# Moving a small transpose, shortening the warm-up and resplitting the last tile in a TensorE-bound kernel

## The chip, the cores and the metric

The kernel runs on one core of a Trainium2 chip. The metric is the device time of one execution in microseconds (us), as the median of several executions. The span that a profile shows is about 1.8 us shorter than the execution's time (177.2 us beside 179.01), because it runs from the first to the last instruction.

Engine names in the profile: PE is TensorE's matmuls, PEld its weight loads, DVE VectorE, ACT ScalarE, POOL GpSimd, SP SyncE, which issues most DMAs. A "q" behind a name is that engine's sequencer. In the views PS is PSUM, the memory that the matmuls write to, and arena the program's buffers in on-chip memory. A load lands when the last of its completions has come.

## The reference, cut to what matters

```python
xn = layernorm(x)                        # x: 2048 x 512, bf16
# part A: a diagonal complex state space model over the sequence
Bu = xn @ B_bar.T                        # B_bar from B_re, B_im and three parameter vectors
h[t] = Lam_bar * h[t-1] + Bu[t]
yA = 2 * real(h @ Cmat.T) + xn * Dskip
# part B: a gated feed-forward layer
yB = (gelu(xn @ w_gate) * (xn @ w_up)) @ w_down     # 512 -> 1376 -> 512
out = x + yA + yB
```

The work goes in four blocks of 512 rows of x (blocks 0 to 3), each of four tiles of 128 rows. The three parameter vectors (12 rows of 128 numbers) must be transposed once, so that a parameter lies in each partition.

## The kernel before: the parts that the change touches

The program lists operations with what they read and write. A scheduler with estimated durations then fixes, before anything runs, the order of the operations on each engine. TensorE and SyncE keep the order of the program; VectorE, ScalarE and GpSimd get an order by priority. Each engine then runs its list strictly in that order, waiting on semaphores.

```python
def params():                              # (before)
    bank = wb                              # the warm-up's PSUM bank
    ...transpose of the 12 parameter rows on TensorE ("Tpar")
    ...VectorE copies 12 columns from PSUM, GpSimd and VectorE compute from them...

def GU_first(fts, early, banks):           # gate and up matmuls of block 0
    ...
    for n in range(2):
        for ft in early:                   # gate, tile 0, 128 columns, 12 matmuls
            mm(ft, 0, 0, 1, [2 * n, 2 * n + 1], toks=[XT0h[n]])
    for ft in early:                       # gate, tile 1, 128 columns, 12 matmuls
        mm(ft, 0, 1, 2)
    params()
    for ft in early:                       # up, tiles 0 and 1, 256 columns
        mm(ft, 1, 0, 2)
    ...

# DN(b, tail=c): the last tile's down matmuls in columns 0:c and c:512:
#   19 matmuls each, then VectorE adds PSUM and skip path, then SyncE stores
...
nwarm = 10                                 # dummies of 512 columns, to get the clock up
...
PE(fwarm, ...)
LN_first()                                 # layernorm of x tiles 0 and 1
TR0(0, "AA")                               # four PE transposes of tile 0, copied by ScalarE
fill(3)                                    # three dummies of 128 columns
hbanks = ...
TR0(1, "V", hbanks[0][4])                  # four PE transposes of tile 1, copied by VectorE
LN(0, [2, 3], True, [GATE["evT"]])
load_B()
GU_first(range(5), range(3), hbanks)
...
DN(3, tail=384)
```

The loads that the head needs are issued by SyncE in this order: x tile 0, x tile 1, gate weights (first chunk, for `early`), x tiles 2 and 3, up weights (first chunk), then second chunks of gate and up.

## Time and profile before

| | before |
|---|---|
| first measurement, 3 runs | 179.05 us (178.86 to 179.4) |
| span of the profiled run | 177.2 us |
| PE busy | 173.1 us, 98% |
| DVE busy | 157.0 us, 89% |
| first up matmul / end of last matmul | 7.72 us / 174.90 us |

The share of PE and the chain of waits, from the page (parts 1 and 4; the shares are of the span):

```profile
PE 173.1 (98%) x902; PEld 86.6 (49%) x917; DVE 157.0 (89%) x277; ACT 91.2 (51%) x175; POOL 11.4 (6%) x23
...
PE 84%; issue 0%; DVE 0%
```

TensorE bounds the kernel: the chain that ends last lies on it. Listed one by one, matmul starts leave no idle time between 11.3 us and the last matmul (some records are missing there). So a change can win only before and after that stretch.

The timeline of PE before, head (start us, length us, engine, line, operation, tiles, shapes, count, and in brackets the idle time before it with what ended it):

```profile
0.99 4.45 PE L937 MATMUL PS<-arena 128*128 128x512 bf16 x10 [0.99 <-DVE arena L525]
5.23 0.49 PE L679 MATMUL PS<-arena 128*128 128x128 bf16 x4
5.56 0.33 PE L943 MATMUL PS<-arena 128*128 128x128 bf16 x3
5.72 0.39 PE L679 MATMUL PS<-arena 128*128 128x128 bf16 x4
6.17 1.50 PE L768 MATMUL PS<-arena 128*128 128x128 bf16 x24
7.61 0.18 PE L547 MATMUL PS<-arena 12*128 12x12 bf16 x1
7.71 2.36 PE L768 MATMUL PS<-arena 128*128 128x256 bf16 x20
```

The lines are dummies, transposes of x tile 0, fillers, transposes of x tile 1, gate matmuls, the parameter transpose, up matmuls. Lengths overlap, since matmuls are pipelined; what counts is the starts. From gate to up there are 24 matmuls that should start 0.056 us apart, 1.34 us together, but the up matmuls start 1.54 us after the gate ones: the parameter transpose between them costs the other 0.20.

The tail before, on VectorE:

```profile
173.97 0.56 DVE L905 TENSOR_TENSOR arena<-PS,arena 128x384 bf16<-128x384 f32 x1 [2.40 <-PE PS L887]
174.93 0.29 DVE L905 TENSOR_TENSOR arena<-PS,arena 128x128 bf16<-128x128 f32 x1 [0.41 <-PE PS L887]
```

VectorE has 0.41 us of idle time between the two additions: with 384 and 128 columns the first addition is done, and its store issued, before the second part is ready.

### The profile page before, as it was taken

To read this page: it belongs to the slowest core of one execution; us is meant where nothing else is said; L and a number is where in the kernel's file an instruction comes from. 1 tells how busy PE (TensorE), PEld (TensorE's weight loads), DVE (VectorE), ACT (ScalarE), POOL (GpSimd) and SP (SyncE) were. 2 spreads that over 40 slices of the span, in tenths; PEclk is the share of its full clock that TensorE was granted. 3 is DMA by queue.
4 is the path that set the end of the run, shared out by engine and by line. 5 is a ranking of instruction groups with operands and counts; after the bars stand their busy time and mean duration, and the time that the engine had idled before them with its cause. 6 is when DMAs were issued, how large, how long until landed. Compare 5 with 4: busy or idle time off the path is not lost.

```text
span 177.2 us, 2507 instructions
## 1 busy us (share of the span) xinstructions
PE 173.1 (98%) x902; PEld 86.6 (49%) x917; DVE 157.0 (89%) x277; ACT 91.2 (51%) x175; POOL 11.4 (6%) x23
## 2 busy tenths in 40 slices
PE   7999999999999999999999999999999999999994
PEld 2787464444644444444644444444464444444453
DVE  5769997997999979979999999899999999999511
ACT  4379999966576898002676793000657960000000
POOL 3210123024000000300000000000000000000000
DMA  4999925997043000001024000000003000001211
GB/s 127 341 246 227 323 59 110 155 267 236 0 90 62 0 0 0 2 30 63 30 59 89 2 0 4 30 30 30 30 0 33 0 0 0 0 0 62 90 52 37
DMA packets 26371, 12.90 MB, mean 73 GB/s; under 512 B 17688, under 2 KB 26360, under 8 KB 26360
## 3 DMA queue, kind: packets, MB, share of 16 engines
q1 hardware_dynamic: 26336, 12.75, 29.5%
q8 instruction: 7, 0.11, 0.3%
q14 instruction: 4, 0.03, 0.1%
q10 hardware_dynamic: 24, 0.00, 0.0%
HBM read 6.46 MB, written 2.10 MB: 48 GB/s over the span
## 4 chain that ended last, share of the span: by engine, by line
PE 84%; issue 0%; DVE 0%
PE PS L887 37%; PE PS L847 33%; PE PS L706 12%; PE PS L821 2%; DVE arena L905 0%
## 5 line engine op out<-in xcount | busy, mean ns | idle before, releaser
L887 PE MATMUL PS<-arena 128*128 128x512 bf16 (+3 forms) x317 | 65.9, 366 | 0.3
L847 PE MATMUL PS<-arena 128*128 128x512 bf16 x273 | 60.7, 379 | 0.4
L887 PEld LDWEIGHTS PS<-arena 128*128 128x128 bf16 (+1 forms) x323 | 30.8, 98 | 35.2
L847 PEld LDWEIGHTS PS<-arena 128*128 128x128 bf16 x280 | 27.3, 98 | 32.1
L739 DVE TENSOR_TENSOR_SCAN arena<-arena 128x512 bf16<-128x512 f32 x32 | 38.9, 1254 | 0.9 <-POOL arena L553 0.9
L862 ACT ACTIVATE arena<-PS 128x512 bf16<-128x512 f32 x35 | 21.1, 602 | 35.6 <-PE PS L847 33.9
L706 PE MATMUL PS<-arena 128*128 128x512 bf16 x126 | 28.0, 379 | 0.1
L865 ACT ACTIVATE arena<-PS 128x512 bf16<-128x512 f32 x35 | 21.0, 602 | 5.3 <-PE PS L847 5.3
L706 PEld LDWEIGHTS PS<-arena 128*128 128x128 bf16 x128 | 12.5, 98 | 14.9
L710 ACT ACTIVATE arena<-PS 128x512 bf16<-128x512 f32 x32 | 17.9, 597 | 2.1 <-PE PS L706 2.0
L905 DVE TENSOR_TENSOR arena<-PS,arena 128x512 bf16<-128x512 f32 (+2 forms) x17 | 10.9, 652 | 9.1 <-PE PS L887 9.0
L879 ACT ACTIVATE PS<-arena 128x512 f32<-128x512 bf16 (+2 forms) x17 | 9.3, 579 | 16.8 <-DVE arena L905 16.5
L867 DVE TENSOR_TENSOR arena<-arena 128x512 bf16<-128x512 bf16 x35 | 13.9, 413 | 1.7 <-ACT arena L865 1.7
L768 PE MATMUL PS<-arena 128*128 128x256 bf16 (+1 forms) x92 | 9.3, 259 | 0.1
L726 DVE TENSOR_TENSOR arena<-arena 128x4096 bf16<-128x4096 bf16 (+1 forms) x5 | 9.3, 1856 | 0.0
L728 DVE TENSOR_TENSOR arena<-arena 128x4096 bf16<-128x4096 bf16 (+1 forms) x5 | 9.3, 1856 | 0.0
L751 DVE TENSOR_TENSOR arena<-arena 128x4096 bf16<-128x4096 bf16 x4 | 9.1, 2283 | 0.0
L752 DVE TENSOR_TENSOR arena<-arena 128x4096 bf16<-128x4096 bf16 x4 | 9.1, 2282 | 0.0
L639 DVE BATCH_NORM_STATS2 arena<-arena 128x6 f32<-128x512 bf16 x14 | 8.9, 679 | 0.1
L768 PEld LDWEIGHTS PS<-arena 128*128 128x128 bf16 x92 | 7.8, 98 | 1.1 <-issue 0.4
L589 DVE SCALAR_TENSOR_TENSOR arena<-arena 128x512 bf16<-128x512 bf16 x8 | 5.5, 742 | 1.2 <-ACT arena L586 1.2
L661 DVE TENSOR_TENSOR arena<-arena 128x512 bf16<-128x512 bf16 x16 | 6.0, 412 | 0.0
(93 smaller groups left out, 111.8 us busy)
## 6 DMA issues: line engine op xcount, KB each, us to landing
out_dram<-arena SPq DMA_DIRECT2D x15, 128.0 KB, 1.7
arena<-in_A_x_dram SPq DMA_DIRECT2D x3, 512.0 KB, 6.9
arena<-in_B_w_down_dram SPq DMA_DIRECT2D x1, 1280.0 KB, 6.9
arena<-in_B_w_gate_dram SPq DMA_DIRECT2D x1, 736.0 KB, 5.8
arena<-in_B_w_up_dram SPq DMA_DIRECT2D x1, 736.0 KB, 7.2
arena<-in_B_w_gate_dram SPq DMA_DIRECT2D x1, 384.0 KB, 3.7
arena<-in_B_w_up_dram SPq DMA_DIRECT2D x1, 384.0 KB, 4.5
arena<-in_A_x_dram SPq DMA_DIRECT2D x2, 128.0 KB, 2.2
```

The lines of the kernel that those rows point to most:

```text
L706: ins_ = e.matmul(PS[bank][:, :], BBT[c][dk].ap[:, 128 * s:128 * (s + 1)], XNT[b].ap[:, dk, :], start=(dk == 0), stop=(dk == KD - 1))
L710: ACT(lambda e, bank=bank, k3=k3, s=s, c=c: e.activation(SSc[k3][s][c].ap, PS[bank][:, :], ACTF.Copy), d_act(512), [BANK[bank]], [SSc[k3][ ...
L726: V(lambda e, s0=s0, s1=s1: e.tensor_tensor(TA.ap[:, s0:s1], ssb.ap[:, s0:s1], cos4[:, s0:s1], ALU.mult), d_dve_tt2x(1024 * step), [ss, CO ...
L728: V(lambda e, s0=s0, s1=s1: e.tensor_tensor(TB.ap[:, s0:s1], ssb.ap[:, s0:s1], sin4[:, s0:s1], ALU.mult), d_dve_tt2x(1024 * step), [ss, SI ...
L739: V(lambda e, g=g, rb=rb, init=init: e.tensor_tensor_scan(g.ap, rb, g.ap, init, ALU.mult, ALU.add), d_dve_scan(512), [g, PA[RRr]] + ([CARc ...
L768: ins_ = e.matmul(PS[bank][:, q0:q0 + 128 * (j1 - j0)], W.ap[:, dk, 128 * ft:128 * (ft + 1)], XNT[0].ap[:, dk, 128 * j0:128 * j1], start=( ...
L847: ins_ = e.matmul(PS[bank][0:m, c0:c1], W.ap[:, dk, 128 * ft:128 * ft + m], XNT[b].ap[:, dk, c0:c1], start=(dk == 0), stop=(dk == KD - 1))
L862: GATE["last_gelu"] = ACT(lambda e, bg=bg, kk=kk, m=m: e.activation(GG[kk].ap[0:m, :], PS[bg][0:m, :], ACTF.Gelu_apprx_tanh), d_act(512), ...
L865: ACT(lambda e, bu=bu, kk=kk, m=m: e.activation(UPB[kk].ap[0:m, :], PS[bu][0:m, :], ACTF.Copy), d_act(512), [BANK[bu]], [UPB[kk]], "evU")
L867: V(lambda e, kk=kk, m=m, ft=ft, k2=k2: e.tensor_tensor(HTt[k2][ft].ap[0:m, :], GG[kk].ap[0:m, :], UPB[kk].ap[0:m, :], ALU.mult), d_dve_tt ...
L887: ins_ = e.matmul(PS[bank][:, c0:c1], l_[:, 128 * j:128 * (j + 1)], r_[:, c0:c1], start=False, stop=last and n == len(ops) - 1, skip_group ...
L905: V(lambda e: e.tensor_tensor(OUTB[ko].ap[:, c0:c1], PS[bank][:, c0:c1], XD[tt].ap[:, c0:c1], ALU.add), d_dve_1x(c1 - c0), [BANK[bank], XD ...
```

## The change

Its intent: start the first x transpose earlier (fewer dummies ahead of it), put the parameter transpose where TensorE waits anyway, and leave less work behind the last matmul.

```diff
-        def params():
-            bank = wb
+        def params(bank):
...
             for ft in early:
                 mm(ft, 0, 1, 2)
-            params()
             for ft in early:
                 mm(ft, 1, 0, 2)
...
-        nwarm = 10
+        nwarm = 9
...
         PE(fwarm, d_pe([512] * nwarm) * 1.6, [WRM], [BANK[wb]], "warm")
+        fill(1)
         LN_first()
         TR0(0, "AA")
-        fill(3)
         hbanks = [{ft: next_bank() for ft in range(5)} for h in range(2)]
+        params(hbanks[0][3])
+        fill(1)
         TR0(1, "V", hbanks[0][4])
...
-        DN(3, tail=384)
+        DN(3, tail=448)
```

## The prediction

> **What bounds the kernel now.** TensorE: the page gives PE 173.1 of 177.2 us busy, and the chain of waits lies on PE for 84% of the span. Matmul starts, listed one by one, show no stall between 11.3 us and the tail (the gaps there are missing records). So only head and tail can move.
>
> **Head, before (timeline, record by record).** Ten dummies start every 0.427 us from 0.99; the clock turns full at about 5.45 (128-column matmuls then start every 56 ns, before it every 107). The first normalised x tile is ready at 4.88 (its weight load starts at 4.94), but its transpose waits behind the dummies until 5.23. The first gate matmul waits for ScalarE's copy of it and starts at 6.17, after 0.23 us of idle PE. The parameter transpose at 7.61 costs 0.26 us from the matmul before it to the one after, where 0.056 is normal: 0.20 lost.
>
> **Head, after.** Nine dummies and one of 128 columns end at about 4.91, so the first x transpose starts at 4.95, ScalarE's copy 0.28 earlier, the first gate matmul at 5.89. The parameter transpose falls into time in which PE waited or filled (the second x tile is ready only at 5.56; three fillers become one), so its 0.20 us is saved. 24 matmuls later, at 7.23 instead of 7.72, PE meets the up weights, which landed at 7.22: they just bind. The up matmuls start at about 7.28: 0.44 gained. What VectorE and GpSimd make of the parameters starts 2.5 us earlier; nothing waits for it. The third and fourth x tiles (ready 9.23 and 9.55) are needed at 9.5 and 9.7: little slack, perhaps 0.1 lost. Head: 0.3 to 0.44 us gained, all on the critical path.
>
> **Tail (timeline).** Before: 19 matmuls of 384 columns every 163 ns, 19 of 128 every 56, the last ending at 174.90; VectorE adds 384 columns in 0.56 us, 128 in 0.29 (1.04 ns a column); SyncE issues a store in 0.33; the last store lands 1.45 us after its issue starts at 175.25. After: 448 columns (189 ns) and 64. If 64-column matmuls start every 29 ns, PE ends as before; if the weight load binds (98 ns warm, 151 cold, a difference that fits 128 columns of clock; the Trainium skill, "TensorE: Matmul & The Clock Gate", section LDWEIGHTS, lets its time go by columns), [...]PE ends 0.2 to 0.5 us later. No run has shown this size yet. Either way VectorE adds 448 columns (0.63 us) until 175.1, SyncE issues that store until 175.45, and the last store goes out at 175.5 or later, where it was 175.25. The tail loses 0.25 to 0.4 us: too little matmul time remains to hide the larger addition and its store issue.
>
> **Sum.** -0.38 + 0.3, about -0.1 us: 178.95 us, range 178.5 to 179.35. Within 2%: 0.98; faster by more 0.01; slower by more 0.01.
>
> **What would show it.** First x transpose near 4.95, first gate matmul near 5.9, up matmuls near 7.3; PE between head and tail unchanged; the last two store issues back to back; 64-column matmuls over 29 ns apart.
>
> **What would make it wrong.** The clock: the same page (Part 1) calls its release window free-running; with fewer dummies it might come a window later, costing over 1 us. A new static order of VectorE's work could delay an x tile. Later up weights would take back head gain. A cheaper tail would give 178.6.

## The result, and the profile after

Six runs of each: 179.51 us after (179.12 to 179.8), 179.11 us before (178.78 to 179.56). The ratio is 1.002, with a 95% interval of 1.0000 to 1.0039. Ratios here are close to the ratio of the mean times, not of the medians. The change makes the kernel about 0.2% (0.36 us) slower, with an interval that just reaches no difference. The prediction had it 0.1 us faster, and at most at 179.35 us. The profiled run after was the slowest of its six (179.8 us), so its head shows a bad case and not a typical one.

The timeline of PE after, head:

```profile
0.99 4.02 PE L935 MATMUL PS<-arena 128*128 128x512 bf16 x9 [0.99 <-DVE arena L525]
4.80 0.31 PE L941 MATMUL PS<-arena 128*128 128x128 bf16 x1
5.04 0.60 PE L678 MATMUL PS<-arena 128*128 128x128 bf16 x4
5.58 0.19 PE L546 MATMUL PS<-arena 12*128 12x12 bf16 x1
5.70 0.28 PE L941 MATMUL PS<-arena 128*128 128x128 bf16 x1
5.78 0.43 PE L678 MATMUL PS<-arena 128*128 128x128 bf16 x4
6.04 1.53 PE L767 MATMUL PS<-arena 128*128 128x128 bf16 x24
8.21 1.48 PE L767 MATMUL PS<-arena 128*128 128x256 bf16 x12 [0.64 <-DMA arena<-in_B_w_up_dram]
```

The first x transpose starts 0.19 us earlier, the gate matmuls 0.13 us earlier, and the parameter transpose has left the space between gate and up. PE has finished the gate matmuls sooner than before, and then waits for the load of the up weights (0.64 us of idle PE by the view; 0.80 us counted from when the next matmul would have started): the up matmuls start at 8.21 us, 0.5 us later than before. The chain of waits after, in order of time, goes back to that load:

```profile
2.18 0.51 SPq L483
2.69 0.04 issue
2.73 5.44 DMA arena<-in_B_w_up_dram
8.17 0.04 issue
8.21 2.36 PE PS L767 x20
```

The tail after, on VectorE:

```profile
174.97 0.76 DVE L903 TENSOR_TENSOR arena<-PS,arena 128x448 bf16<-128x448 f32 x2 [2.91 <-PE PS L885]
```

The view merges the two additions (0.63 and 0.22 us) because nothing lies between them any more: VectorE is still adding the first 448 columns when the last matmul ends at 175.39 us.

One identity makes the rest easy. From the start of the first up matmul to the end of the last matmul both profiles take 167.18 us. So span = start of the first up matmul + 167.18 + tail, where the tail is the time from the end of the last matmul to the end of the span. Before: 7.72 + 167.18 + 2.26. After: 8.21 + 167.18 + 2.59. In the profiled runs the head lost 0.50 us and the tail 0.33.

### The profile page after: what moved, and what is told of

It reads as the page before. It is cut to its first block, busy times and chain, and to the rows that moved or that the text cites. A ratio compares the mean times of both kernels' runs of the same rounds, so it can differ in the third digit from the quotient of the medians.

```text
span 178.0 us, 2518 instructions
## 1 busy us (share of the span) xinstructions
PE 173.8 (98%) x915; PEld 86.0 (48%) x915; DVE 157.3 (88%) x277; ACT 91.6 (51%) x175; POOL 10.9 (6%) x23
## 4 chain that ended last, share of the span: by engine, by line
PE 94%; DMA 3%; SPq 1%; DVE 0%; issue 0%; DVEq 0%
PE PS L885 37%; PE PS L845 34%; PE PS L705 16%; PE PS L767 4%; DMA arena<-in_B_w_up_dram 3%; PE PS L819 3%; SPq L479 0%; DVE arena L903 0%; SPq L483 0%; SPq L475 0%; PE PS L678 0%; DVEq L374 0%; DVEq L340 0%
## 5 line engine op out<-in xcount | busy, mean ns | idle before, releaser
L845 PE MATMUL PS<-arena 128*128 128x512 bf16 x280 | 61.7, 379 | 0.0
L705 PE MATMUL PS<-arena 128*128 128x512 bf16 x128 | 28.3, 379 | 0.0
```

Source lines behind the costliest of these rows:

```text
L705: ins_ = e.matmul(PS[bank][:, :], BBT[c][dk].ap[:, 128 * s:128 * (s + 1)], XNT[b].ap[:, dk, :], start=(dk == 0), stop=(dk == KD - 1))
L845: ins_ = e.matmul(PS[bank][0:m, c0:c1], W.ap[:, dk, 128 * ft:128 * ft + m], XNT[b].ap[:, dk, c0:c1], start=(dk == 0), stop=(dk == KD - 1))
```

## The experiments

Theory A: the two parts add up; the tail costs 0.3 us in every run, and the head wins little because the up weights land at about the time at which PE now wants them. Rivals: fewer dummies delay the release of the clock (B); the tail is free and one late load is the whole story (C); the change itself delays that load (D).

The first four runs were on one chip. "Before" had 11 runs there, median 178.96 us.

### The head alone

```diff
 # the changed kernel
-        DN(3, tail=448)
+        DN(3, tail=384)
```

> The head of the change alone: one dummy fewer, fill matmuls rearranged, parameter transpose between the first two x transposes; last tile split in 384 and 128 as before. Theory A (the two parts add up; the tail costs 0.3 us in every run, the head gains little because the up weights land at about the time at which PE now asks for them): 0.0 to 0.35 us faster than before, ratio 0.998 to 1.000, first up matmul at 7.4 us or later and tied to the landing of the up weights. Theory B (fewer dummies let the clock turn full later, so the head itself loses): 0.1 us or more slower than before, with 128-column matmuls still 0.107 us apart after 5.7 us. Tail, from the end of the last matmul to the end of the span, 2.26 us as before in both.

Measured: 179.00 us, ratio 0.9997 (0.9979 to 1.0014). Up weights landed at 7.506 us, first up matmul 7.553, tail 2.27. The clock came as late as about 6.0 us here, and still the run was not slower than before. Theory A's range holds; B's loss of 0.1 us is not seen, though the interval does not exclude it. Nor does it exclude the predicted gain: 0.9979 would be 0.38 us faster.

### The tail alone

```diff
 # the kernel before
-        DN(3, tail=384)
+        DN(3, tail=448)
```

> The tail of the change alone: last tile split in 448 and 64 columns, head as before. Theory A: 0.30 to 0.35 us slower than before (ratio 1.0018), the head unchanged, 64-column matmuls 0.029 us apart, the last store issued right behind the one of 448 columns, from the end of the last matmul to the end of the span 2.59 us instead of 2.26. Theory C (the tail is free, and the later end in the profile after is only the late up weights): within 0.1 us of before.

Measured: 179.33 us, ratio 1.0016 (0.9998 to 1.0034), tail 2.59 us. The 64-column matmuls started 0.029 us apart. The ratio alone does not exclude C, but the tails in the profiles do: all four with 448 and 64 columns, this one included, have 2.58 or 2.59 us, and all nine with 384 and 128 have 2.26 or 2.27. The size of the whole change's loss is that of the tail, as A says; C falls.

### Before and after once more

> The kernel before, unchanged, as one more sample of the noise and of the landings: ratio 1.000 within 0.001; the up weights landing anywhere from 7.1 to 8.2 us if their landing is chance (theory A), near 7.2 us if the change had made it late (theory D).

Measured: 179.07 us, ratio 1.0001 (0.9982 to 1.0019). Up weights landed at 7.32 us, the first up matmul started at 7.42. What surprised was the head: PE ran

```profile
0.99 3.88 PE L937 MATMUL PS<-arena 128*128 128x512 bf16 x10 [0.99 <-DVE arena L525]
4.94 0.40 PE L679 MATMUL PS<-arena 128*128 128x128 bf16 x4
...
5.85 1.53 PE L768 MATMUL PS<-arena 128*128 128x128 bf16 x24
7.31 0.18 PE L547 MATMUL PS<-arena 12*128 12x12 bf16 x1
```

with the *ten* dummies of the kernel before. The clock had become full at about 4.2 us instead of 5.4, so the last dummies took half the time and x tile 0 was the later one. The first transpose then starts at 4.94 us without the change.

> The changed kernel, unchanged: ratio about 1.002 again, as 1.0018 of the tail and about 1.000 of the head. If the up weights' late landing at 8.17 us was chance (theory A), it lands earlier here, most likely 7.2 to 7.6 us, and the first up matmul starts within 0.05 us of it; if the change causes it (theory D), again near 8.2 us. Clock full at 5.4 to 5.9 us.

Measured: 179.36 us, ratio 1.0017 (0.9996 to 1.0038). Here the up weights landed early, at 7.137 us, and the first up matmul started at 7.212. D, with its repeat near 8.2 us, is not borne out; late landings are not a constant of the change. (The expectation had 7.2 to 7.6 us and a clock that is full at 5.4 to 5.9 us; it was full at 3.8.) But the gain was not kept: from first up to last matmul PE took 167.51 us instead of 167.18. It waited 0.16 us for the next gate chunk (landed 8.63 us) and 0.17 us near 32 us. The cause of the second is in the timeline of DVE, first of this run:

```profile
19.36 2.47 DVE L638 BATCH_NORM_STATS2 arena<-arena 128x6 f32<-128x512 bf16 x4
...
23.46 1.29 DVE L638 BATCH_NORM_STATS2 arena<-arena 128x6 f32<-128x512 bf16 x2 [0.96 <-DMA arena<-in_A_x_dram]
24.67 0.15 DVE L647 RECIPROCAL arena<-arena 128x2 f32<-128x2 bf16 x1
24.85 0.74 DVE L652 TENSOR_SCALAR arena<-arena 128x512 bf16<-128x512 bf16 x2
```

then of the kernel before, in the run above:

```profile
19.63 1.28 DVE L639 BATCH_NORM_STATS2 arena<-arena 128x6 f32<-128x512 bf16 x2
...
22.61 0.41 DVE L653 TENSOR_SCALAR arena<-arena 128x512 bf16<-128x512 bf16 x1
```

The change gave the scheduler other start times for the parameters' arithmetic, and it made another static order for VectorE. (This was checked by running the kernel's own scheduler without the chip: with the parameter transpose alone moved it makes this new order (except for the split of the tail); with the dummies and fillers alone changed it keeps the order of before.) In the new one, statistics of block 2 (a load that lands at 22.6 to 24.6 us in the profiles with this order) stand *before* the normalisation of block 1 (the TENSOR_SCALAR lines). So block 1 waits for a load that it does not need. Its DMA transposes were issued from 25.3 us here and from 23.05 us before, and landed last at 32.10 instead of 29.41 us. The second B projection, which needs them, is due at about 32.2 us.

### The head with the order of before

Theory E: the head's gain is capped twice, first by the landing of the up weights, later by this order. To test it, the schedule of before was kept and only TensorE's list and the 12-column copy were changed by hand:

```diff
 # the kernel before
-            for _ in range(nwarm):
+            for _ in range(nwarm - 1):
                 ...dummy of 512 columns
+            ...one dummy of 128 columns
...
-                for _ in range(n):            # fill(3)
+                for _ in range(n - 2):
...
-        def params():
-            bank = wb
+        def params(bank):
...
-            params()
+            params(banks[0][3])
...
         S.schedule()
+        # in TensorE's list: parameter transpose moved ahead of the fillers
+        # in VectorE's list: the 12-column copy moved ahead of the first x copy
```

The next four runs were on one chip, with "before" at 178.99 us (11 runs, 178.73 to 179.53).

> The head of the change with VectorE's, ScalarE's and GpSimd's order of before (only the copy of the 12 parameter columns moves), last tile 384 and 128. Theory E (the head gain is capped twice: first by the landing of the up weights, later, at the second B projection near 32 us, by the transposes of the second x block, which the new static order of VectorE issues about 2 us later): the transposes land last at 29.3 to 29.8 us as before (30.8 to 32.1 in the head change with its own order), the first up matmul at the landing of the up weights plus 0.05 us or at 7.2 to 7.45 us, whichever is later; 0.05 to 0.2 us faster than before, ratio 0.9990 to 0.9997. Rival (order without effect, landing the only cap): the transposes land as in the head change alone.

Measured: 179.21 us, ratio 1.0005 (0.9991 to 1.0019). The time missed theory E's range. In the profiled run the up weights landed at 8.055 us and the first up matmul started at 8.102, as late as in the first profile after. Block 1's transposes landed last at 30.08 us, outside the range named, since the head was late; counted from the first up matmul it is 21.98 us, as in the two profiles of before (21.99 both). The first of these transposes was issued 1.02 us after block 2's load had landed (and 0.17 us ahead of it in the run with 416 columns below); in the four profiles with the new order it is 1.85 to 2.04 us after it every time.

In the profile the up matmuls waited for the load once more:

```profile
8.10 1.59 PE L767 MATMUL PS<-arena 128*128 128x256 bf16 x13 [0.64 <-DMA arena<-in_B_w_up_dram]
```

The landing is now the suspect. The next kernel takes its wait away, by letting every gate and up matmul of the first block read gate weights that are there anyway; the result is wrong:

```diff
 # the run above
-     ins_ = e.matmul(..., W.ap[:, dk, 128 * ft:128 * (ft + 1)],
+     ins_ = e.matmul(..., WG.ap[:, dk, 128 * (ft % 3):128 * (ft % 3 + 1)],
...
+        # after S.schedule(): these matmuls keep of the weight loads only the first
```

> The same, with every gate and up matmul of the first x block reading the first gate weights, so that none waits for a later weight load; the result is wrong on purpose. Theory E: first up matmul 1.34 us after the first gate matmul (at 7.2 to 7.45 us), without any tie to the landing of the up weights, no stall up to the tail; 0.2 to 0.35 us faster than before, ratio 0.9980 to 0.9989. If the landing is no cap: same time as with the weights waited for.

Measured: 178.63 us (178.5 to 178.88), ratio 0.9975 (0.9962 to 0.9988), a little better than expected. The first up matmul started at 7.255 us, 1.36 us after the first gate matmul at 5.891, while the up weights landed only at 7.484. PE shows gate and up matmuls as one row without idle time:

```profile
5.89 3.27 PE L769 MATMUL PS<-arena 128*128 128x128 bf16 x40
```

From the first up matmul to the last matmul: 167.17 us. This run and the one before it differ only in which weights are read, and so in the waits for them; their intervals do not overlap, and the waits cost the new head 0.30% (about 0.5 us). That this run is also 0.45 us faster than before looks like the 0.44 us that the prediction had seen in the head, but it is a coincidence: the kernel before still waits for weights in this comparison. A later run takes its waits away too.

> Again no wait for the later weights (wrong on purpose), but with the change's own static order. Theory E: VectorE waits for the third x block's load near 22.5 to 23.5 us with the normalisation of the second x block behind it, the transposes of the second block land last at 30.8 to 32.1 us, and in runs where that is over about 31.8 us the second B projection stalls; slower by 0 to 0.3 us than the run with the old order, ratio to before 0.9983 to 1.0000. If the order does not matter: the same time as with the old order within 0.05 us and no stall near 32 us.

Measured, with the same edit on the changed kernel (tail 384): 179.02 us (178.66 to 179.96), ratio 1.0000 (0.9979 to 1.0021). The gain is gone, though none of the first block's weights is waited for; the loss against the old order, 0.4 us, is more than the 0.3 expected. The profiled run was the slowest of the six and shows how: block 2's load landed at 24.6 us, later than in any other profile, and block 1's transposes at 33.2, after the range named. Its chain of waits:

```profile
16.16 8.47 DMA arena<-in_A_x_dram
24.65 1.29 DVE arena L638 x2
26.04 0.73 DVE arena L652 x2
...
32.49 0.34 DVE arena L867
33.02 0.50 ACT arena L862
33.52 4.04 PE PS L705 x18
```

It no longer lies on PE: it comes from block 2's load over VectorE's queue and ScalarE to PE, which lost 1.4 us between 30 and 33.5 us (168.58 us from first up to last matmul). The two intervals overlap slightly, so the size in the mean is uncertain; that the order can cost is shown by this chain.

### A tail between the two

> The head of the change with the order of before and the last tile split in 416 and 96 columns: a candidate for a faster kernel. Tail from the last matmul's end to the end of the span 2.23 us (2.26 with 384 and 128, 2.59 with 448 and 64), head as with the old order: 0.1 to 0.25 us faster than before, ratio 0.9987 to 0.9995, within the noise of the timing.

The edit is the head with the order of before and `tail=416`. Measured: 179.06 us, ratio 1.0000 (0.9985 to 1.0015). The up weights landed at 7.708 us. The tail was 2.33 us, not 2.23. The last store was indeed issued 0.03 us earlier after the last matmul than with 384 and 128, but its issue took 0.43 us instead of 0.33. It landed 1.54 us after its issue instead of 1.45. No candidate for a faster kernel.

### Which part of the tail costs

The next three runs were on another chip, with "before" at 179.22 us (11 runs, 178.74 to 179.48).

```diff
 # the kernel before, tail=448
-  ..., is_output=True, tag="st_out")
+  ..., is_output=True, tag="st_out", queue="scalar" if c0 else "sync")
```

> The tail of the change alone (448 and 64 columns), but the very last store is issued by ScalarE's queue, which is idle then, instead of standing behind the store of the 448 columns on SyncE. Theory F (the tail loses because the two stores are issued one behind the other, 0.33 and then 0.43 us, right after VectorE's longer addition): the last store's issue starts within 0.1 us of the end of VectorE's 64-column addition instead of 0.27 us after it; from the last matmul's end to the end of the span 2.30 to 2.45 us instead of 2.59; 0.05 to 0.2 us slower than before. Rival G (VectorE's longer addition alone costs the 0.3 us): still 2.55 us or more.

Measured: 179.33 us, ratio 1.0006 (0.9991 to 1.0021). The last store's issue started 0.03 us after its addition, as theory F wanted, but the tail stayed at 2.58 us. Measured from the end of the last matmul:

| | addition of the large part ends | its store issued, landed | last store issued, landed |
|---|---|---|---|
| 384 + 128 (before) | -0.37 | -0.34, 1.29 | 0.36, 1.80 |
| 448 + 64 (tail alone) | 0.20 | 0.23, 1.92 | 0.60, 2.12 |
| 448 + 64, last store from ScalarE | 0.20 | 0.23, 1.95 | 0.37, 2.12 |

The ratio, 0.1 us slower, would fit F, and it is lower than the 1.0016 of the tail with SyncE's queue, but that was measured on another chip, and the intervals hold each other's value; the tails in the profiles agree. F falls by the tail. What fits is G in this form: the longer addition makes the *large* store late. It takes 1.7 us from issue to landing, and with 448 columns it can be issued only when VectorE has added them, 0.57 us later than with 384. Already this store lands at 1.92 us or later, after the very last one of before (1.80). The small one lands just behind it whoever issues it. From ScalarE's queue it took 1.75 us from issue to landing instead of 1.51; whether that is because it runs behind the large one or because of the other queue, these runs do not separate. So of the 0.32 us by which the last landing moved (1.80 to 2.12), 0.12 us is shown to be the large store's own lateness (1.92); that the small one's landing behind it belongs to the same cause is argued.

### What before itself loses, and the parts of the head

The same edit as above (no wait for the later weights), on the kernel before:

> The kernel before, with all gate and up matmuls of the first x block reading the first gate weights (wrong on purpose), so that none waits for a later load. Theory H (the up weights land so variably that the kernel before already waits for them in many runs): first up matmul at 7.42 to 7.72 us, no run over 179.15 us (before goes to 179.6), ratio to before 0.9985 to 0.9995. Rival: the kernel before never waits for them, ratio 0.9998 to 1.0002 with the same spread.

Measured: 178.78 us (178.69 to 179.2), ratio 0.9985 (0.9967 to 1.0003). One run was 0.05 us over the bound that the expectation named. The mean points to H, that the kernel before already waits for the up weights in part of its runs, but the interval does not exclude that it never does. The profile: first up matmul at 7.511 us, with the weights landing at 7.636. In that very run the real kernel would have waited. This is the fair partner of the new head without waits (0.9975): between the two without waits only 0.0010 is left for the head itself, 0.18 us instead of 0.44, on different chips and with intervals that overlap.

> The same without waits for weights (wrong on purpose), with ten dummies and three fillers as before, but the parameter transpose moved ahead of the fillers, VectorE's order as before. If the move is worth the 0.20 us that the transpose costs at its old place: 0.15 to 0.25 us faster than the kernel before without waits, first up matmul 1.34 us after the first gate matmul; what then remains to the run with all of the new head and no waits (ratio 0.9975) is the dummies' share, 0 to 0.15 us, as the clock turned full at 3.7 to 4.2 us in four of seven profiles and the dummies then end before the first x tile is ready.

Measured: 178.85 us (178.49 to 179.13), ratio 0.9981 (0.9965 to 0.9998). The difference from the run before, 0.0004 or 0.07 us where 0.15 to 0.25 was expected, cannot be told from noise. Its profile fell on a clock that became full only at 6.33 us, with the gate matmuls at 6.495. The up matmuls followed 1.365 us after them where the kernel before has 1.54 to 1.57: the parameter transpose's 0.20 us is gone from there. But in this run it came back at the new place: the gate matmuls started 1.27 us after the first x transpose, where the kernel before, with a late clock too, has 0.95. How the head's gain divides in time between move and dummies stays open.

### An attempt to get the weights earlier

```diff
 # the head with the order of before, after S.schedule()
+  # the first gate chunk's load: from SyncE's list to ScalarE's, second there
```

> A candidate that goes at the cap: the head of the change with the order of before, last tile 384 and 128, and the first gate weights' load issued from ScalarE's queue (second there, at about 1.3 us) instead of SyncE's third place, so that SyncE issues the second half of x and the up weights 0.5 us earlier. If the landing of the up weights is the cap of the head and follows the time of issue: it lands 0.2 to 0.5 us earlier than in the head with SyncE's loads alone (7.1 to 8.2 us in the profiles so far), first up matmul at 7.2 to 7.6 us, 0.1 to 0.4 us faster than before (ratio 0.9978 to 0.9995). If the DMA engines are simply full from 3 us on, or the first x tiles land later: no change or slower by up to 0.3 us.

Measured, on a chip with before at 179.01 us: 179.18 us (seven runs, 179.0 to 180.92), ratio 1.0009 (0.9992 to 1.0025). In the one profile the up weights landed at 7.39 us, inside the range of the others, though issued 0.6 us earlier. The profiled run was the one of 180.92 us:

```profile
0.99 4.02 PE L936 MATMUL PS<-arena 128*128 128x512 bf16 x9 [0.99 <-DVE arena L525]
...
6.26 0.16 PE L546 MATMUL PS<-arena 12*128 12x12 bf16 x1 [0.46 <-DMA arena<-in_A_Lambda_im_dram]
6.36 0.29 PE L943 MATMUL PS<-arena 128*128 128x128 bf16 x1
6.43 0.63 PE L678 MATMUL PS<-arena 128*128 128x128 bf16 x4
6.86 5.12 PE L767 MATMUL PS<-arena 128*128 128x128 bf16 x44
```

Two things went wrong. The parameter loads, pushed back on ScalarE's queue, landed at 6.1 us, and the parameter transpose stands in PE's list in front of all that follows the first x transposes. And the clock stayed at half: 128-column matmuls started 0.107 us apart until after 9.3 us. Only one run of seven was so slow, and the ratio fits the other six: the plain means of all runs listed give 1.002. None of the kernels with right results beat the kernel before clear of noise.

## Why the prediction was wrong, point by point

**What bounds the kernel, and that only head and tail can move.** The first half was right. The second held in the profile before and in the first one after (167.18 us each), but not in general. The prediction said of the parameters' arithmetic that "nothing waits for it". Directly that is so; but moving it gave VectorE another static order, and that couples block 1 to block 2's load. It cost 0.17 us in one profile and 1.4 us in another, and nothing in the two others with this order (167.18 us both). The words "a new static order of VectorE's work could delay an x tile" stood among the risks; it delayed x block 1, not the tiles of the head.

**First x transpose at 4.95 us, 0.28 earlier.** It started at 5.04, as the first x tile itself was ready 0.1 us later in that run (its load landed at 2.88 us instead of 2.78). Worse, the 0.28 was not the typical gain. The profile before had caught a late clock. In nine of the fourteen profiles the clock was full before 4.7 us; where the kernel had ten dummies among these, its first transpose started at 4.94 to 5.22 us, and with nine at 4.94 to 5.03. In the pair of repeats with an early clock the gate matmuls started at 5.852 us before and at 5.849 after. Dropping dummies pays only where the clock is late.

**The parameter transpose's 0.20 us is saved.** Right for its old place: the gap between gate and up matmuls is gone, and without waits for weights up starts 1.36 us after gate. That the new place is free holds only where the clock is early: there the gate matmuls start 0.91 to 0.99 us after the first x transpose with either kernel. With a late clock it is 0.95 us before, but 1.00 us in the first profile after and 1.08 in the head alone.

**Up matmuls at 7.28 us, 0.44 gained.** This is the step that failed. The prediction put the first up matmul at 7.28 us; it measured 8.21, as PE waited for the up weights. It had taken their landing, 7.22 us, from one profile as if it were a constant, and found that they "just bind". Over the thirteen profiles that load it from SyncE's queue it was 7.14, 7.22, 7.32, 7.37, 7.48, 7.51, 7.56, 7.64, 7.68, 7.69, 7.71, 8.06 and 8.17 us: 7.22 is the second earliest, the median is 7.56. In the first profile after, 15 of the load's 16 completions had come by 7.30 us and the last came at 8.17; one packet of its size took 0.87 us, where the mean of this size was 0.048. The other landing over 8 us had the same form: 15 by 7.36, the last at 8.06.

An estimate from these numbers: before wants the weights at about 7.58 us (mean start of its up matmuls in five profiles), the new head at about 7.32 (where it did not wait, and 1.37 us after gate where it did). If up starts at the later of that and landing plus 0.05 us, the mean over the thirteen landings is 7.72 us before and 7.65 after: 0.07 us gained instead of 0.38. So the estimate loses about 0.18 of the predicted 0.44 us because before is usually faster than its first profile (7.58 instead of 7.72), and about 0.19 to the waits. The measured ratio of the head alone, 0.9997, fits that and does not resolve it; the same head with the old order (0.9991 to 1.0019) does exclude 0.38. That waits for weights take time from the new head is shown by the run without them (0.9975 against 1.0005). How much the head would gain without any waits, 0.18 us by the two runs without them, is not resolved.

Whether the change makes the load land later is not settled. The seven profiles with nine dummies average 7.68 us, the six with ten 7.47, and the two sets overlap.

**Tail: 0.25 to 0.4 us lost.** Right in size: 0.33 us in the profiles, ratio 1.0016. The 64-column matmuls started 0.029 us apart, so the weight load did not bind. The reason was half right. Additions and stores are too late, as said; but it is not the last store's place in SyncE's queue, since giving it another queue left the tail at 2.58 us. The store of 448 columns alone lands after everything that before stores; the rest of the tail's loss is the small store behind it, whose reason stays open.

**The clock.** The risk named was real, and was not what decided here. The release was late in the first profile after (about 5.85 us) and in the head alone (6.0), and early (3.8) in the repeat of the same changed kernel. The Trainium skill, "TensorE: Matmul & The Clock Gate", Part 1, says that the window is free-running and 3.4 us long. The traces fit this and do not show a window itself: the release came at 3.6 to 6.3 us in thirteen profiles, a spread of 2.7 us, and in the fourteenth, with nine dummies, at about 9.8 us, 3.5 us beyond the latest of the others. Early and late releases occur with nine dummies and with ten (3.8 to 9.8 and 3.6 to 6.3 us), so whether fewer dummies make a late one likelier is not settled.

**The sum.** -0.38 + 0.3 should have been about -0.07 + 0.33, by the estimate above and the measured tail. The measured difference, 0.36 us from the ratio, has the size of the tail's 0.33, with about nothing from the head.

## What to carry to other kernels

When a change makes an engine ask earlier for data, the landing of that data is a distribution and not a number: take it from several profiles, and expect that the mean of the later of two times moves less than the one that was moved. After moving even a tiny operation in a program with a static scheduler, compare every engine's order with the old one, because an unrelated load can end up in front of work that was ready. When the last tile is split, the large part's addition and the issue of its store should be through before the small part's matmuls are: with 128 columns that was so here (tail 2.26 us), with 96 and with 64 it was not (2.33 and 2.59).

## What the Trainium skill lacked or had wrong

- "DMA: Bandwidth & Descriptors" gives a fixed part and a rate for a DMA's time (fitted for DMAs that GpSimd issues), but no spread between runs of one load. The same 384 KB load, in the same place of the queue, landed between 7.14 and 8.17 us, once twice held up by one of its 16 completions alone.
- "TensorE: Matmul & The Clock Gate", section Back-to-back issue gap, gives about 81 ns per matmul for a sustained stream of load and matmul pairs of 128 columns and 131 ns for 512, and keeps about 56 and 216 ns for an isolated matmul. Here the pairs in a stream started 56 ns apart at 128 columns, 216 at 512, 189 at 448 and 29 at 64 columns.
- The same page, section LDWEIGHTS, gives, by its formula, 128/1.2 = 107 ns for this weight load. The traces show it 98 ns long at full clock and 147 to 152 at half; at 64 columns pairs start every 29 ns, so the loads overlap here and their length is no bound.
- No page that was read for this says that a store issued right behind another on SyncE's queue costs more to issue than one alone: its issue took 0.43 us (gap to the one before 0.04 us) where one that stood alone took 0.33.
